# A new stored order of all five engines for a linear-attention and Fourier-mixing kernel

## The chip, the cores and the metric

The kernel runs on one core of a Trainium2 chip. Its metric is the time of one execution on the device in microseconds. The core has five engines that run on their own and meet through semaphores: TensorE (PE in the profile; its weight loads are PEld), VectorE (DVE), ScalarE (ACT), GpSimd (POOL) and SyncE (SP). SP issues nearly all transfers; POOL issues those of the two weight matrices.

## The reference, cut to what matters

```python
def _attn_ref(r, k, v, w, u):            # r, k, v, w: (4, 8, 768, 48); u: (8, 48)
    state = np.zeros((B, H, D, D))
    for t in range(S):
        cur = np.einsum('bhd,bhe->bhde', u[None] * kt, vt)
        y[:, :, t] = np.einsum('bhd,bhde->bhe', rt, state + cur)
        state = wt[:, :, :, None] * state + np.einsum('bhd,bhe->bhde', kt, vt)
    return y

def _moe_ref(x, w_ch1, w_ch2):           # x: (4, 768, 384), heads laid side by side
    X = np.fft.fft(np.fft.fft(x, axis=1), axis=2)
    u = x + np.real(X)
    un = (u - mean(u)) / np.sqrt(var(u) + 1e-06)      # over the last axis
    return u + np.maximum(un @ w_ch1, 0.0) @ w_ch2    # 384 -> 1536 -> 384
```

## The kernel before, in words

Four batches are worked one after another through the same stages, and the stages of neighbouring batches overlap.

*Attention.* The 768 steps of a batch are cut into six chunks of 128, one step per partition. For a chunk the decay w is turned into logarithms (ACT), summed over the steps by a matmul with a triangular matrix, and exponentiated (ACT). r and k are scaled by these (the tiles `rkh`, written by VectorE or POOL), transposed into `rkt` (by TensorE and an eviction, or by a transfer), and multiplied with each other (line 1120). A mask makes `ah` of the scores (line 1130, VectorE). The output of the chunk is `ah` times the values `vb` plus the transposed r times the state `st` (lines 1182 and 1185), plus the value times the scalar `dc`, the sum of r·k·u over a head: two products `rk` (VectorE or POOL), a reduction and a scaling `vtd`. The state goes from chunk to chunk (lines 1154, 1157, 1165).

Batch 0 is worked in pairs of chunks: its w, k and r come as three transfers of 384 KB for two chunks each (line 648); values, and all inputs of the other batches, come chunk by chunk in 192 KB (line 654). For each pair, `vec(2 * DM, tt(rk, rt, kt, ALU.mult), ...)` makes the product of r and k, in the profile `uf<-in_r,in_k` or `ht<-in_r,in_k` with 768 elements.

*Fourier mixing.* The outputs of chunks are folded with their mirror (tiles `sd` and `xf`, line 600 on VectorE or POOL), multiplied with tables of cosines and sines (lines 1261 to 1266), evicted to `hcs` with a mirrored copy `hcr`, and multiplied with tables of the second transform (line 1305, or 1314 in four parts). Input and result make `uf`; the normalized rows `un` are transposed to `unt`.

*The layer.* `unt` times W1 (line 1412, 288 matmuls) is evicted with a relu to `ht` (lines 1418 on VectorE and 1420 on ACT), and `ht` times W2 (line 1431) is evicted to `osb` and sent out. Half a batch is worked at a time.

*What sets the order.* The program first records every operation with a number, its reads and writes, the engines that may do it, and alternative forms of some steps (`choose`). A table of numbers, `ORDER`, then says for every engine which operations it does and in which order: `schedule` puts each operation on the engine in whose list its number stands, drops the forms that stand in no list, and gives PSUM banks; `emit` places the semaphore waits. Each engine works its list strictly from first to last. An operation of POOL also waits for the last VectorE instruction ahead of it in the plan that has two SBUF operands or could run in a faster mode.

At the very start TensorE has filler: sixteen matmuls on a tile of ones (line 1464) and `NW` more (line 1507). Ahead of the real work VectorE and ACT make masks and the tables of cosines and sines.

The names that matter below: line 600 is the helper for all elementwise operations on two tiles (`vec`), so VectorE's and POOL's shares of it are told apart by tile; line 639 is the load of u; line 402 and such are waits.

Of the kernel before, what the change touches and what calls it, by code (L numbers as in the profile page):

```python
# [31 lines left out]

W_AFTER = {"W1_0": (0, 4, "w")}

NW = 8

MEANS = (0,)


ORDER = {  # L40
# [26 lines left out]
    "act": (  # L67
# [15 lines left out]
    "dve": (  # L83
# [17 lines left out]
    "pool": (  # L101
# [13 lines left out]
}  # L115


# [335 lines left out]
def bass_rwkv6_finch__then__fnet_fourier_mix_kernel(  # L453
# [1048 lines left out]
    g.ctx = "warm"  # L1502
    for i in range(NW):
        t = g.tile("w")
# [36 lines left out]
```

## Time and profile before

| | |
|---|---|
| time, median of three runs | 179.47 us (179.09 to 179.93) |
| the profiled execution: time, span | 179.5 us, 177.3 us |
| PE busy | 171.9 us, 97% of the span |
| DVE busy | 157.8 us, 89% |
| ACT busy | 132.5 us, 75% |
| POOL busy | 98.4 us, 55% |
| PE clock granted | 1.000 |
| HBM read and written | 23.59 and 4.72 MB |

Times in the profile are microseconds from the start of the span. A busy engine is one that executes instructions; TensorE's matmuls overlap, so its busy time can hide gaps that are shorter than a matmul's way through the array. Idle time of an engine matters only where another engine waits for it.

### The profile page before, as it was taken

The numbers are of one execution on the slowest core, as the hardware profiler recorded it, in microseconds if no ns is written. First come the engines' busy times: TensorE is split into PE (matmuls) and PEld (weight loads), VectorE is DVE, ScalarE is ACT, GpSimd is POOL, SyncE is SP. The second block draws the span as 40 slices with busy tenths as digits, with TensorE's granted clock in tenths as the row PEclk, the third lists the DMA queues.
The fourth block names the chain that finished last, engine by engine and source line by source line (L and its number), as shares of the span: only waits on it lengthen the run. The fifth ranks groups of instructions, "written<-read, shape, count | busy, mean of one in ns | idle before, by whom it ended". The sixth has DMA issues, their size and how long they took to land.

```text
span 177.3 us, 4554 instructions
## 1 busy us (share of the span) xinstructions
PE 171.9 (97%) x1704; PEld 114.4 (65%) x1704; DVE 157.8 (89%) x379; ACT 132.5 (75%) x323; POOL 98.4 (55%) x127
## 2 busy tenths in 40 slices
PE   6998999999999999999999999999999999999994
PEld 3366667866766667776667667666666775665663
DVE  8979999999999999999999998999888999683443
ACT  2899999999999986999996988897924573602400
POOL 4024359759989557599589428899376124000000
DMA  5999999999999999997998969989983123240033
GB/s 131 296 276 246 211 202 190 184 177 215 188 186 163 161 186 217 211 208 151 205 191 168 239 134 207 171 150 243 210 174 102 50 89 67 46 154 4 0 133 133
DMA packets 109031, 29.55 MB, mean 167 GB/s; under 512 B 104273, under 2 KB 109010, under 8 KB 109010
## 3 DMA queue, kind: packets, MB, share of 16 engines
q1 hardware_dynamic: 107394, 26.91, 71.5%
q0 software_dynamic: 1616, 2.36, 8.5%
q8 instruction: 13, 0.21, 0.5%
q14 instruction: 8, 0.07, 0.1%
HBM read 23.59 MB, written 4.72 MB: 160 GB/s over the span
## 4 chain that ended last, share of the span: by engine, by line
PE 85%; DVE 6%; SPq 4%; DMA 3%; issue 1%; DVEq 0%
PE bank L1431 27%; PE bank L1412 27%; PE bank L1305 5%; PE bank L1261 3%; PE bank L1120 3%; DMA in_k<-in_k_dram 3%; SPq L648 3%; PE bank L1185 2%; PE bank L1182 2%; PE bank L992 2%; DVE rkh L600 2%; PE bank L1157 2%; PE bank L1109 2%; PE bank L1097 1%; DVE ah L1130 1%; PE bank L1015 1%
## 5 line engine op out<-in xcount | busy, mean ns | idle before, releaser
L1412 PE MATMUL bank<-unt,w 128*128 128x384 bf16 x288 | 53.5, 326 | 0.0
L1431 PE MATMUL bank<-w,ht 128*128 128x384 bf16 (+2 forms) x300 | 53.2, 320 | 0.0
L1420 ACT ACTIVATE ht<-bank 128x384 bf16<-128x384 f32 x75 | 35.2, 505 | 16.2 <-PE bank L1412 16.0
L1431 PEld LDWEIGHTS bank<-w,ht 128*128 128x128 bf16 x300 | 27.7, 98 | 15.7 <-issue 0.2
L1412 PEld LDWEIGHTS bank<-unt,w 128*128 128x128 bf16 x288 | 26.7, 98 | 15.7 <-DVE rkh L1046 0.2
L1130 DVE TENSOR_TENSOR ah<-bank,msk 128x512 bf16<-128x512 f32 x47 | 30.3, 678 | 1.6 <-PE bank L1120 1.3
L600 POOL TENSOR_TENSOR rk<-rk,ub 128x384 f32<-128x384 f32 x15 | 15.0, 1000 | 5.1 <-DVE rk L600 2.6
L1418 DVE TENSOR_SCALAR ht<-bank 128x384 bf16<-128x384 f32 x21 | 10.8, 548 | 7.0 <-PE bank L1412 7.0
L1440 DVE SCALAR_TENSOR_TENSOR osb<-bank,rstd,uf 128x384 f32<-128x384 f32 (+2 forms) x22 | 13.0, 591 | 4.0 <-DMA out_dram<-osb 2.4
L623 ACT ACTIVATE rkt<-bank 128x512 bf16<-128x512 bf16 (+1 forms) x22 | 15.5, 711 | 1.2 <-PE bank L1109 0.8
L614 ACT ACTIVATE un<-uf,agg 128x384 bf16<-128x384 f32 x22 | 12.8, 618 | 3.9 <-DVE agg L1364 3.9
L600 POOL TENSOR_TENSOR rkh<-in_k,e 128x384 bf16<-128x384 f32 x13 | 13.0, 1007 | 4.6 <-DVE xf L600 2.4
L600 POOL TENSOR_TENSOR vtd<-in_v,dc 128x384 f32<-128x384 f32 x17 | 14.0, 828 | 0.8 <-DVE dc L1064 0.7
L614 ACT ACTIVATE vb<-in_v 128x384 bf16<-128x384 f32 x23 | 12.3, 543 | 2.8 <-DMA in_v<-in_v_dram 2.8
L600 POOL TENSOR_TENSOR rk<-in_r,in_k 128x384 f32<-128x384 f32 x11 | 11.0, 1008 | 2.9 <-DVE xf L600 2.8
L1185 PE MATMUL bank<-vb,ah 128*128 128x48 bf16 x192 | 11.1, 183 | 0.0
L1185 PEld LDWEIGHTS bank<-vb,ah 128*128 128x128 bf16 x192 | 9.7, 96 | 1.6 <-issue 0.4
L600 POOL TENSOR_TENSOR sd<-x 128x385 f32<-128x385 f32 x8 | 8.0, 1008 | 4.6 <-DVE rkh L600 1.9
L1196 DVE TENSOR_TENSOR x<-bank,vtd 128x384 f32<-128x384 f32 x18 | 9.8, 547 | 0.8 <-PE bank L1185 0.5
L614 ACT ACTIVATE lb<-in_w 128x384 bf16<-128x384 f32 x18 | 9.8, 544 | 0.7 <-PE bank L992 0.4
L1362 DVE BATCH_NORM_STATS2 bst<-uf 128x6 f32<-128x384 f32 x18 | 9.6, 547 | 0.2 <-POOL uf L600 0.2
L1064 DVE TENSOR_REDUCE dc<-rk 128x8 f32<-128x384 f32 x18 | 9.7, 541 | 0.0
(208 smaller groups left out, 392.0 us busy)
## 6 DMA issues: line engine op xcount, KB each, us to landing
in_v<-in_v_dram SPq DMA_DIRECT2D x24, 192.0 KB, 4.4
out_dram<-osb SPq DMA_DIRECT2D x23, 192.0 KB, 2.6
in_w<-in_w_dram SPq DMA_DIRECT2D x18, 192.0 KB, 3.9
in_r<-in_r_dram SPq DMA_DIRECT2D x18, 192.0 KB, 3.8
in_k<-in_k_dram SPq DMA_DIRECT2D x18, 192.0 KB, 4.1
in_r<-in_r_dram SPq DMA_DIRECT2D x3, 384.0 KB, 4.4
in_k<-in_k_dram SPq DMA_DIRECT2D x3, 384.0 KB, 4.5
in_w<-in_w_dram SPq DMA_DIRECT2D x3, 384.0 KB, 5.4
```

The lines of the kernel that those rows point to most:

```text
L600: return lambda e: e.tensor_tensor(out=o, in0=a, in1=b, op=f)
L614: return lambda e: e.activation(o, a, f, **kw)
L623: {"act": lambda e: e.activation(o(), i(), ACTF.Copy), "dve": lambda e: e.tensor_copy(out=o(), in_=i())}, **kw)
L1064: op("dve", v_1(DM), lambda e: e.tensor_reduce(out=dc[:, :], in_=rku[:, :, :], axis=mybir.AxisListType.X, op=ALU.add), r=[("RK", i2)], w=[ ...
L1130: masked[n].append(op("dve", v_1(512), lambda e: e.tensor_tensor(out=ah[:, x:H:2, :], in0=ps(bk)[:, :].rearrange("p (h t) -> p h t", t=128 ...
L1185: ins = e.matmul(ps(ty)[:, D * h:D * h + D], ah[:, h, :], vb[:, h, :], start=first and not ype, stop=True, skip_group_check=True)
L1196: op("dve", v_1(DM), lambda e: e.tensor_tensor(out=xb[:, c, 0:DM], in0=ps(ty)[:, 0:DM], in1=vflat, op=ALU.add), r=[ty, ("VTD", n % 4)], w= ...
L1412: ins = e.matmul(ps(t)[:, 0:384], W1[:, m, 256 * (j // 2) + j % 2:256 * (j // 2) + 256:2], unt[:, :, m, :], start=(m == 0), stop=(m == NM ...
L1418: {"dve": lambda e, j=j, t=t, ht=ht: e.tensor_scalar(out=ht[:, j, :], in0=ps(t)[:, 0:384], scalar1=su, scalar2=0.0, op0=ALU.mult, op1=ALU. ...
L1420: "act": lambda e, j=j, t=t, ht=ht: e.activation(ht[:, j, :], ps(t)[:, 0:384], ACTF.Relu, scale=su)},
L1431: ins = e.matmul(ps(t)[:, 0:hi - lo], ht[:, j, 128 * x:128 * x + 128], W2[:, j, lo:hi], start=(j == 0), stop=(j == NJ - 1))
L1440: op("dve", v_1(hi - lo) + 64, lambda e: e.scalar_tensor_tensor(out=o[:, lo:hi], in0=ps(t)[:, 0:hi - lo], scalar=rstd[:, kb:kb + 1], in1=u ...
```

## The change

The table `ORDER` is replaced by another, and `NW` goes from 8 to 9. Everything else is the same text. The new table holds the lists of the five engines in another order, moves some operations to another engine, and picks another form for eight steps. It came from a search over the order, judged on mildly disturbed courses of the program's own plan.

```diff
-NW = 8
+NW = 9
 ORDER = {
     "pe": (
-        "8 84 2367 2368 2369 2370 2371 2372 2373 2374 105 108 101 208 211 204 102 77 138 157 151 152 155 147 "
...
+        "8 84 2367 2368 2369 2370 2371 2372 2373 2374 2375 108 105 101 211 208 204 102 77 155 138 157 151 152 "
...
     "sp": (
-        "87 83 86 82 90 88 92 91 95 89 97 93 96 636 638 687 98 94 789 99 738 689 637 639 845 688 690 790 739 "
...
+        "87 86 83 82 90 91 88 92 93 89 95 97 689 96 94 789 636 99 687 738 98 638 639 637 845 688 690 741 790 "
...
```

The steps with another form: the scaled k of chunks 2 and 3 (two operations of one chunk each become one of both), the sums of w for chunks 4 and 5 (one of the two running sums goes on in the bank of the first), the evictions of three transposes (two of 512 become one of 1024 for chunks 2 and 4 of batch 1, the reverse for chunk 1 of batch 2), the scaled r of chunk 5 of batch 3, the addition for chunk 1 of batch 3, and the output of the fourth block of batch 0.

The first place is the head of SP's queue. 128x8x96 is a transfer for two chunks of batch 0, 128x8x48 one for one chunk, 1x384 is u. Before:

```order
L648 DMA in_r<-in_r_dram 128x8x96
L639 DMA osb<-in_u_dram 1x384
L648 DMA in_k<-in_k_dram 128x8x96
L648 DMA in_w<-in_w_dram 128x8x96 x2
L654 DMA in_v<-in_v_dram 128x8x48
L648 DMA in_r<-in_r_dram 128x8x96
L648 DMA in_k<-in_k_dram 128x8x96
L648 DMA in_w<-in_w_dram 128x8x96
L654 DMA in_v<-in_v_dram 128x8x48
L648 DMA in_r<-in_r_dram 128x8x96
```

Now (the file is one line shorter, so lines count one less):

```order
L647 DMA in_r<-in_r_dram 128x8x96
L647 DMA in_k<-in_k_dram 128x8x96
L638 DMA osb<-in_u_dram 1x384
L647 DMA in_w<-in_w_dram 128x8x96 x2
L647 DMA in_k<-in_k_dram 128x8x96
L653 DMA in_v<-in_v_dram 128x8x48
L647 DMA in_r<-in_r_dram 128x8x96
L653 DMA in_v<-in_v_dram 128x8x48 x2
L647 DMA in_w<-in_w_dram 128x8x96
L647 DMA in_r<-in_r_dram 128x8x96
```

The k of chunks 0 and 1 now stands ahead of u, the k of chunks 2 and 3 ahead of the values of chunk 0 and of its own r, and the values of chunks 2 and 1 ahead of the w of chunks 4 and 5.

The second place is POOL's list in batch 3, around the scaled k of chunk 4 (`rkh<-in_k,e_1`). Before:

```order
L600 TENSOR_TENSOR rk<-in_r,in_k 128x384
L600 TENSOR_TENSOR rk<-rk,ub 128x384
L600 TENSOR_TENSOR uf<-uf,xf 128x191
L600 TENSOR_TENSOR rk<-rk,ub 128x384
L600 TENSOR_TENSOR uf<-uf,xf 128x191
L600 TENSOR_TENSOR rkh<-in_k,e_1 128x8x48
L600 TENSOR_TENSOR vtd<-in_v,dc 128x384 x2
L600 TENSOR_TENSOR x<-x,vtd 128x384
L600 TENSOR_TENSOR rk<-rk,ub 128x384
L600 TENSOR_TENSOR sd<-x 128x385
```

Now:

```order
L599 TENSOR_TENSOR uf<-uf,xf 128x191
L599 TENSOR_TENSOR vtd<-in_v,dc 128x384 x2
L599 TENSOR_TENSOR uf<-uf,xf 128x191
L599 TENSOR_TENSOR rk<-in_r,in_k 128x384
L599 TENSOR_TENSOR rk<-rk,ub 128x384
L599 TENSOR_TENSOR rk<-in_r,in_k 128x384
L599 TENSOR_TENSOR rkh<-in_k,e_1 128x8x48
L599 TENSOR_TENSOR x<-x,vtd 128x384
L599 TENSOR_TENSOR rk<-rk,ub 128x384
L599 TENSOR_TENSOR rk<-in_r,in_k 128x384
L599 TENSOR_TENSOR vtd<-in_v,dc 128x384
L599 TENSOR_TENSOR sd<-x 128x385
```

The products of r and k for chunks 4 and 5 of batch 3, which VectorE made before, now stand in POOL's list, one of them ahead of the scaled k of chunk 4, and two scalings `vtd` that stood behind it stand ahead of it.

133 rows, old and new, of the table ORDER are left out of this document.

## The prediction

> **What bounds the kernel now.** I read the head of the page first, then who TensorE waited for, then a table by stage, and last the chain of waits.
>
> ```profile
> span 177.3 us, 4554 instructions
> PE 171.9 (97%) x1704; PEld 114.4 (65%) x1704; DVE 157.8 (89%) x379; ACT 132.5 (75%) x323; POOL 98.4 (55%) x127
> ```
>
> TensorE is busy for 171.9 of 177.3 us. The profiled execution took 179.5 us, so 2.2 us lie around the span; the median of the runs is 179.47, which is the same. All sums below are made against 179.5. The view of waits lists everything for which TensorE's matmuls stood idle (who waited, for whom, us in total, times, longest):
>
> ```profile
> PE bank L1464 <- DVE w L611: 1.4, 1, 1.4
> PE bank L913 <- DVE sml L906: 0.3, 1, 0.3
> PE bank L1507 <- DVE msk L604: 0.3, 1, 0.3
> PE bank L942 <- DVE rkh L600: 0.3, 1, 0.3
> PE bank L1205 <- DVE vtd L600: 0.2, 1, 0.2
> PE bank L857 <- ACT uf L614: 0.2, 1, 0.2
> ```
>
> That is 2.7 us in all. The first 1.4 us stand ahead of the sixteen filler matmuls of line 1464, so no work of the kernel is late by them. The other lines all belong to batch 0 and the tables. The stages say the same (busy us of PE, weight loads, DVE, ACT, POOL in each stretch, then granted clock, DMA share and GB/s):
>
> ```profile
> 20.00:30.00 10.00, 9.86 (x141) 7.19 (x143) 10.00 (x19) 9.79 (x24) 6.68 (x13) 1.00 1.05 195
> 30.00:60.00 30.00, 29.99 (x360) 20.95 (x360) 29.37 (x74) 29.58 (x75) 25.52 (x31) 1.00 1.03 184
> 90.00:120.00 30.00, 30.00 (x341) 20.21 (x340) 28.82 (x63) 26.27 (x63) 22.46 (x25) 1.00 0.90 181
> 150.00:178.00 28.00, 24.80 (x165) 15.44 (x163) 14.10 (x31) 5.96 (x15) 0.59 (x1) 1.00 0.25 76
> ```
>
> From 30 us on TensorE has nothing left to win, and VectorE (DVE) runs within 0.63 us of full in 30 to 60 and within 1.18 us in 90 to 120. A new order of the same work can therefore gain almost only in the first 30 us, and can lose anywhere. The chain of waits tells what sets the opening (start, us, what), and how the end stands:
>
> ```profile
> 7.28 5.40 DMA in_k<-in_k_dram
> ...
> 13.64 1.02 DVE rkh L600 x2
> ...
> 24.24 0.48 DVE st L1165
> ...
> 146.17 5.20 PE bank L1431 x32
> ...
> 167.62 7.19 PE bank L1431 x56
> 174.91 0.35 DVE osb L1440
> ```
>
> The opening hangs on the eighth transfer of SP's queue, the keys of chunks 2 and 3. After it comes one unbroken string of VectorE instructions until 24.24. From there the chain is TensorE's, up to the last output.
>
> **The change part by part.** No computation goes. The count of TensorE's matmuls hardly moves: two fewer at line 857 and one more at line 863 for chunks 4 and 5, and one more filler at line 1507.
>
> *The opening transfers.* VectorE stands idle twice before 13 us, both times for keys:
>
> ```profile
> 6.16 0.96 DVE L600 TENSOR_TENSOR uf<-in_r,in_k 128x768 f32<-128x768 f32 x1 [0.32 <-DMA in_k<-in_k_dram]
> ...
> 10.85 0.96 DVE L600 TENSOR_TENSOR rkh<-in_k,uf 128x768 bf16<-128x768 f32 x1
> 12.77 0.96 DVE L600 TENSOR_TENSOR ht<-in_r,in_k 128x768 f32<-128x768 f32 x1 [0.96 <-DMA in_k<-in_k_dram]
> ```
>
> SP issues them like this:
>
> ```profile
> 1.25 0.47 SPq L639 DMA_DIRECT2D osb<-in_u_dram  x1
> 1.78 0.40 SPq L648 DMA_DIRECT2D in_k<-in_k_dram  x1
> ...
> 4.75 1.30 SPq L654 DMA_DIRECT2D in_v<-in_v_dram  x1
> 6.09 1.15 SPq L648 DMA_DIRECT2D in_r<-in_r_dram  x1
> 7.28 1.11 SPq L648 DMA_DIRECT2D in_k<-in_k_dram  x1
> ```
>
> The change issues the first keys ahead of the small load of u, at 1.25 instead of 1.78, 0.53 earlier. That can take away the first wait of 0.32, but alone it gives nothing: VectorE would then only stand longer at the second. For the second, the same eight transfers are ahead; the keys now go before the values and the receptances r of chunks 2 and 3, so r is the eighth. The lower bound of the gain is nothing, if the eighth lands at 12.68 (7.28 and 5.40) whatever it is. For the upper, the view of DMA issues has the median time from issue to landing in the first 16 us:
>
> ```profile
> in_r<-in_r_dram SPq DMA_DIRECT2D x3, 384.0 KB, 4.4
> in_w<-in_w_dram SPq DMA_DIRECT2D x3, 384.0 KB, 5.4
> in_v<-in_v_dram SPq DMA_DIRECT2D x3, 192.0 KB, 4.5
> ```
>
> An r issued at 7.28 with 4.4 lands at 11.68, before VectorE is free (10.85 and 0.96 is 11.81). Then both waits go: 0.32 and 0.96 are 1.28. Between 0 and 1.28 I take 0.6, about the middle, since the bytes ahead are the same, and the 5.40 of this transfer against the usual 4.4 shows that it was late for a reason I can't see. The string of VectorE behind it holds the same work: up to the product of chunk 5 with its mask, at 31 us, VectorE's instructions differ by one tiny scaling taken from ACT and a few fills. So the gain goes on to TensorE.
>
> *What the transfers push back.* The first values, now seventh, are issued about where r stood, at 6.09, and land with 4.5 at 10.6. The decay w of chunks 4 and 5 goes from ninth to eleventh place behind two more small loads; issued two places later, where the trace issues at 10.51, it lands with 5.4 at 15.9. ACT uses them here:
>
> ```profile
> 10.44 0.53 ACT L614 ACTIVATE vb<-in_v 128x384 bf16<-128x384 f32 x1
> ...
> 10.51 2.17 SPq L648 DMA_DIRECT2D in_r<-in_r_dram  x1
> ...
> 15.65 0.83 ACT L614 ACTIVATE uf<-in_w 128x768 bf16<-128x768 f32 x1
> ```
>
> So ACT may wait 0.16 and 0.25, and behind the first wait stand the exponentials that the products of chunks 0 and 1 need. I count 0.1 on the path; bounds are 0 (the products wait for r anyway) and 0.4.
>
> *Forms and fillers.* A matmul of 384 columns leaves every 0.163 us (32 in 5.20). One fewer of them at lines 857 and 863 and one more filler at 1507 cancel. The filler stands where TensorE waits for line 857 anyway; with that cover gone it would cost its 0.163. Sum 0.
>
> *Work moved from VectorE to POOL.* Counted over both programs, the products r times k go from 7 on VectorE and 11 on POOL to 3 and 15, one sum of two chunks and one addition of 191 columns move too.
>
> ```profile
> L600 POOL TENSOR_TENSOR rk<-in_r,in_k 128x384 f32<-128x384 f32 x11 | 11.0, 1008 | 2.9 <-DVE xf L600 2.8
> ...
> L600 DVE TENSOR_TENSOR rk<-in_r,in_k 128x384 f32<-128x384 f32 x7 | 3.8, 548 | 0.0
> ...
> L600 POOL TENSOR_TENSOR uf<-uf,xf 128x191 f32<-128x191 f32 x8 | 4.7, 590 | 5.6 <-DVE uf L1353 2.9 <-DVE uf L600 2.6
> ```
>
> POOL gets about 5 times 1.0 and 0.6, which is 5.6 us; VectorE loses 4 times 0.548, about 0.55 for the sum and 0.36 for the addition, 3.1 us. Nearly all of it lies after 70 us, where TensorE never waits, so the gain there is close to 0. POOL is 55% busy; in 90 to 120 it has 7.5 us free. What hides the longer POOL instructions is that the products are wanted only by the reduction to dc and the scaled values, which the output of a chunk needs last. I take 0, with a gain of 1.5 (half of the relief, if VectorE is the hidden bound) and a loss of 1.5 (below) as bounds.
>
> What POOL can cost is seen where its instruction meets one of VectorE that also reads two tiles of SBUF:
>
> ```profile
> 147.60 0.36 DVE L600 TENSOR_TENSOR uf<-uf,xf 128x191 f32<-128x191 f32 x1
> ...
> 148.83 1.14 POOL L600 TENSOR_TENSOR uf<-uf,xf 128x191 f32<-128x191 f32 x2 [0.20 <-DVE uf L1353]
> ...
> 149.46 0.72 DVE L600 TENSOR_TENSOR uf<-uf,xf 128x191 f32<-128x191 f32 x1
> ```
>
> The same addition took 0.36 alone and 0.72 while POOL was busy until 149.97: VectorE was held. The Trainium skill, page "SBUF — State Buffer", section "Who interferes with whom", has the rule: a VectorE instruction with two SBUF inputs and a GpSimd instruction that reads SBUF exclude each other for the whole instruction, and whoever comes first goes first. This row agrees with it. By that rule each moved product is a stretch of 1.0 in which such VectorE work stands still, which speaks against the change; it is the first rival.
>
> *The turn to batch 3 and the end.* The 32 matmuls from 146.17 bridge the time in which batch 3 is normalized and transposed. In the new order the same nine groups of four output matmuls (32 in that row and four just before it) bridge it again. The last 7.19 us of TensorE are one run of output matmuls before and after. I count 0 for both.
>
> **Sum.** 179.5 minus 0.6 plus 0.1 is 179.0 us.
>
> **The rivals.** *POOL holds VectorE.* About six more POOL instructions stand where VectorE is nearly full. Each that meets a two-input instruction costs 0.36 (the row) to 1.0. Four meetings at 0.36 are about 1.5, past the 0.6 gained, and TensorE waits for masks and sums. Time: 179.0 and 1.5, 180.5. For it: no slack on VectorE between 30 and 120. Against: the relief of 3.1 us, and POOL's idle times before its products show that the order already keeps the two apart. It decides from two meetings on the path.
>
> *Both keys' waits go.* r lands after 4.4 and ACT's loads come in time: 179.5 minus 1.28 is 178.2. For it: 4.4 is the median. Against: the engines of the DMA are full.
>
> *VectorE was the bound of the middle.* Then half of the 3.1 us, 1.5, comes off beside the 0.6 and the 0.1: 177.5. For it: 29.37 of 30. Against: no wait of TensorE there.
>
> *The new order does nothing for the time.* The eighth transfer lands as before and the rest cancels: 179.5.
>
> **How the numbers follow.** What a measurement can tell from no change is about 0.5%, 0.9 us. Forecast 179.0, own range 178.5 to 179.5: 0.37. POOL holds VectorE, 180.5: 0.21. Both waits go, 178.2: 0.20. VectorE's bound, 177.5: 0.10. Nothing, 179.5: 0.12. Faster by over 0.9 us are the third (most of it) and the fourth, and a little of the first: 0.33. Slower are most of the second and a tail of the last: 0.22. The rest, 0.45, is the same. The range from 177.6 to 180.8 reaches into the two outer cases.
>
> **What would show it.** The product r times k of chunks 2 and 3 (VectorE, 12.77 now) starts at 11.5 to 12.5, and the string behind it is as long as now; if it starts at 12.7 the first term is wrong. ACT's first conversion of v starts no later than 10.8. TensorE's waits after 30 us stay under 0.3; VectorE's additions and products that read two tiles stay at 0.55, and longer ones mean the first rival. The wait before batch 3's first matmul of line 1412, at 151, stays away. A new wait of TensorE between 30 and 150 of more than half a microsecond would make the prediction wrong.

## The result and the profile after

| | before | after |
|---|---|---|
| time, median of six runs | 179.32 us (178.88 to 179.93) | 178.13 us (177.88 to 178.17) |
| after over before, 95% interval | | 0.9932 (0.9914 to 0.9949) |
| the profiled execution: time, span | 179.5, 177.32 us | 178.16, 176.35 us |
| what lies around the span | 2.2 us | 1.8 us |

The change is faster by 1.2 us, 0.7%. The forecast was 179.0 with a range from 177.6 to 180.8, and 178.1 lies inside it. It lies outside the 178.5 to 179.5 that the prediction gave to its own course of things, and beside the rival at 178.2. The head of the page of the changed kernel, and all of its waits of TensorE's matmuls:

```profile
span 176.3 us, 4538 instructions
PE 171.6 (97%) x1704; PEld 114.4 (65%) x1704; DVE 155.7 (88%) x372; ACT 133.0 (75%) x324; POOL 103.7 (59%) x131
```

```profile
PE bank L1463 <- DVE w L610: 1.3, 1, 1.3
PE bank L856 <- ACT uf L613: 0.6, 1, 0.6
```

The first wait is the one ahead of the fillers. The second is new in its size, but stands ahead of line 856 with fillers on its other side; the logarithms that it waits for come at the same time as before, so nothing is late by it. After 30 us no wait is left, as before. Now VectorE's start of the program (start, us, the instruction; what ended a wait would stand in brackets):

```profile
5.55 0.19 DVE L603 TENSOR_SCALAR msk<-osb 128x128 bf16<-128x128 f32 x1
...
5.87 0.93 DVE L599 TENSOR_TENSOR uf<-in_r,in_k 128x768 f32<-128x768 f32 x1
...
10.82 0.94 DVE L599 TENSOR_TENSOR rkh<-in_k,uf 128x768 bf16<-128x768 f32 x1
...
11.69 0.95 DVE L599 TENSOR_TENSOR ht<-in_r,in_k 128x768 f32<-128x768 f32 x1
...
30.82 0.54 DVE L1164 TENSOR_TENSOR st<-bank,sml 128x384 bf16<-128x384 f32 x1
```

Both waits for keys are gone. The product of r and k of chunks 2 and 3 (`ht<-in_r,in_k`, called the product below) starts at 11.69 instead of 12.77, directly behind the instruction before it. The string behind it holds: the last update of batch 0's state starts at 30.82, and stood at 31.80 before:

```profile
31.80 0.54 DVE L1165 TENSOR_TENSOR st<-bank,sml 128x384 bf16<-128x384 f32 x1
```

The chain of waits of the changed kernel shows that TensorE carries this to the end. Its first row here ends with the landing of r at 11.18, 0.5 us before the product that reads it, so no engine stood for it:

```profile
6.57 4.61 DMA in_r<-in_r_dram
...
145.20 5.20 PE bank L1430 x32
...
166.44 7.41 PE bank L1430 x56
```

The 32 output matmuls that bridge the turn to batch 3 start at 145.20 instead of 146.17, and the last run of TensorE ends at 173.85 instead of 174.81: 0.96 earlier, the whole of the 1.0 us that the span lost. Three of the stages shown in the prediction say that the middle is as full as it was:

```profile
20.00:30.00 10.00, 9.99 (x141) 6.84 (x140) 10.00 (x21) 10.00 (x26) 6.78 (x11) 1.00 1.05 188
30.00:60.00 30.00, 29.95 (x356) 21.33 (x355) 29.49 (x70) 29.85 (x79) 25.60 (x32) 1.00 1.06 191
90.00:120.00 30.00, 30.00 (x351) 20.35 (x350) 28.98 (x62) 25.86 (x64) 22.75 (x26) 1.00 1.06 180
```

In the profiled executions, then, 1.0 us of the gain lies in the opening, and 0.4 us lies around the span (0.3 us by the medians below).

### The profile page after: what moved, and what is told of

The parts are those of the page before. It is cut to its first block, busy times and chain, and to the rows that moved or that the text cites. A ratio compares the mean times of both kernels' runs of the same rounds, so it can differ in the third digit from the quotient of the medians.

```text
span 176.3 us, 4538 instructions
## 1 busy us (share of the span) xinstructions
PE 171.6 (97%) x1704; PEld 114.4 (65%) x1704; DVE 155.7 (88%) x372; ACT 133.0 (75%) x324; POOL 103.7 (59%) x131
## 4 chain that ended last, share of the span: by engine, by line
PE 87%; DVE 4%; SPq 3%; DMA 3%; issue 1%; DVEq 0%
PE bank L1430 27%; PE bank L1411 27%; PE bank L1304 5%; PE bank L1119 4%; PE bank L1260 4%; DMA in_r<-in_r_dram 3%; PE bank L1184 3%; SPq L647 2%; PE bank L1181 2%; PE bank L1204 2%; PE bank L1156 2%; PE bank L991 2%; PE bank L1108 2%; PE bank L1265 1%; PE bank L1014 1%; DVE ah L1129 1%
## 5 line engine op out<-in xcount | busy, mean ns | idle before, releaser
L1419 ACT ACTIVATE ht<-bank 128x384 bf16<-128x384 f32 x74 | 33.8, 494 | 10.8 <-PE bank L1411 10.5
L1439 DVE SCALAR_TENSOR_TENSOR osb<-bank,rstd,uf 128x384 f32<-128x384 f32 (+2 forms) x23 | 13.5, 593 | 7.7 <-PE bank L1430 7.4
L599 POOL TENSOR_TENSOR rk<-in_r,in_k 128x384 f32<-128x384 f32 x15 | 15.0, 1002 | 4.7 <-DVE rk L599 2.4
L1417 DVE TENSOR_SCALAR ht<-bank 128x384 bf16<-128x384 f32 x22 | 11.6, 547 | 6.3 <-PE bank L1411 5.9
L622 ACT ACTIVATE rkt<-bank 128x512 bf16<-128x512 bf16 (+1 forms) x21 | 14.8, 740 | 2.5 <-PE bank L1108 2.5
L599 POOL TENSOR_TENSOR sd<-x 128x385 f32<-128x385 f32 x9 | 8.9, 1009 | 1.7 <-DVE x L1195 1.1
L1181 PE MATMUL bank<-st,rkt 128*128 128x96 bf16 x80 | 9.7, 204 | 0.0
L1195 DVE TENSOR_TENSOR x<-bank,vtd 128x384 f32<-128x384 f32 x17 | 9.2, 548 | 0.4 <-PE bank L1184 0.3
```

Source lines behind the costliest of these rows:

```text
L599: return lambda e: e.tensor_tensor(out=o, in0=a, in1=b, op=f)
L622: {"act": lambda e: e.activation(o(), i(), ACTF.Copy), "dve": lambda e: e.tensor_copy(out=o(), in_=i())}, **kw)
L1181: e.matmul(ps(ty)[:, 96 * q:96 * q + 96], rT[:, q, :], s_in[:, q, :], start=not ype, stop=False, skip_group_check=True)
L1417: {"dve": lambda e, j=j, t=t, ht=ht: e.tensor_scalar(out=ht[:, j, :], in0=ps(t)[:, 0:384], scalar1=su, scalar2=0.0, op0=ALU.mult, op1=ALU. ...
L1419: "act": lambda e, j=j, t=t, ht=ht: e.activation(ht[:, j, :], ps(t)[:, 0:384], ACTF.Relu, scale=su)},
L1439: op("dve", v_1(hi - lo) + 64, lambda e: e.scalar_tensor_tensor(out=o[:, lo:hi], in0=ps(t)[:, 0:hi - lo], scalar=rstd[:, kb:kb + 1], in1=u ...
```

## The experiments

Line numbers in the experiments' profiles are 12 above those of before (14 in the two with fills of an unused tile; the changed kernel run again has its own). Besides its median, each kernel is told by the median span of its executions and by what the device time has beyond the span, since the two move apart. Times of before in the three sets were 179.39, 179.41 and 179.46 us. Four single executions are left out: one of 608 us in the second run with both keys early, one of 183.9 us in the run with the second keys and the mask, and two of before in the first set, 181.2 and 183.1 us (the 179.39 still counts these two).

### Which transfer gives the gain

In SP's list, 87 and 86 are r and k of chunks 0 and 1, 83 is u, 82 and 90 are the w, 88 the first values, 92 and 91 r and k of chunks 2 and 3. Both keys early, in the order of before:

```diff
-        "87 83 86 82 90 88 92 91 95 89 ...
+        "87 86 83 82 90 91 88 92 95 89 ...
```

> The order of before, with only the head of SP's queue taken from the change: both keys early. Theory A (the head of SP's queue is the whole gain): VectorE has 0.32 + 0.96 us of waits to lose, and no other one appears, so the product of r and k of chunks 2 and 3 starts at 11.7 to 11.9 instead of 12.77 and the time falls by 0.9 to 1.1 us. Theory B (the gain needs the new lists of the other engines too: VectorE's lists of the first 12 us were written for the old landings): the product may start as early, but the time falls by less than 0.5 us, because other waits open between 12 and 30 us.

Measured: 178.53 us, ratio 0.9954 (0.9938 to 0.9969), median span 176.4 against 177.2. VectorE has no wait left ahead of the product:

```profile
11.53 0.95 DVE L612 TENSOR_TENSOR ht<-in_r,in_k 128x768 f32<-128x768 f32 x1
```

Only the first keys:

```diff
-        "87 83 86 82 90 88 92 91 95 89 ...
+        "87 86 83 82 90 88 92 91 95 89 ...
```

> The order of before, with only the first keys put ahead of the small load of u. Theory A1 (the small load in second place holds the whole stream of transfers back: the first keys landed at 6.07 in the profile of before and at 5.35 in that of after, 0.72 earlier): everything behind lands 0.5 to 0.7 us earlier, the second keys at 12.0 to 12.2, and the time falls by 0.5 to 0.7 us. Theory A2 (of the prediction: alone it gives nothing, VectorE only stands longer at the second keys): second keys at 12.6 to 12.7, time as before within 0.2 us.

Measured: 178.84 us, ratio 0.9973 (0.9952 to 0.9993), median span 176.7.

Only the second keys:

```diff
-        "87 83 86 82 90 88 92 91 95 89 ...
+        "87 83 86 82 90 91 88 92 95 89 ...
```

> The order of before, with only the second keys moved ahead of the values and the r of chunks 2 and 3, so that r is the eighth transfer. If the eighth transfer lands when it lands, whatever it is: r at 12.7, product at 12.8, time as before within 0.2 us. If the eighth was late for a reason of its own (5.40 us against 4.4 for r), r lands at about 11.7 to 12.0 and the time falls by 0.6 to 0.9 us; the wait of 0.32 for the first keys stays in both cases.

Measured: 179.37 us, ratio 1.0001 (0.9974 to 1.0029). The twelve executions spread from 178.44 to 180.34: five lie from 178.4 to 178.9, where both keys early lie, and six from 179.5 to 180.3.

And the other way, the changed kernel with the old head of the list:

```diff
-        "87 86 83 82 90 91 88 92 93 89 ...
+        "87 83 86 82 90 88 92 91 93 89 ...
```

> The changed kernel, with only the first eight transfers of SP in the old order. Theory A (the head is the whole gain): both waits of VectorE come back, the product starts at 12.6 to 12.8, and the time is 0.9 to 1.2 us above the changed kernel, level with before. Theory C (the other lists gain by themselves, by half of the work taken from VectorE): the time stays 0.3 us or more below before.

Measured: 178.87 us, ratio 0.9974 (0.9949 to 0.9999), median span 177.05. Its profile is of the longest of the twelve executions (179.27). Both waits are back in it:

```profile
6.52 0.96 DVE L612 TENSOR_TENSOR uf<-in_r,in_k 128x768 f32<-128x768 f32 x1 [0.57 <-DMA in_k<-in_k_dram]
...
12.91 0.96 DVE L612 TENSOR_TENSOR ht<-in_r,in_k 128x768 f32<-128x768 f32 x1 [0.61 <-DMA in_k<-in_k_dram]
```

By the spans, the head of the list is worth about 0.8 us alone (177.2 to 176.4), and 0.7 us when it is taken out of the change (from 176.3 and 176.4 in the two runs of the changed kernel, on other chips, to 177.05). So it is nearly all that the span gained. The profiles say the same more closely. In eleven of the thirteen profiled executions (without the one of 608 us) the span is 164.5 to 164.9 us longer than the start of the product, whether that stands at 11.5 or at 12.9. The two others are the run with products taken back to VectorE (165.5) and the one with fills on POOL (165.2), both described below. The changed kernel with the old head is still 0.5 us below before, but 0.3 of this lies around the span; the fourth part takes that up.

The first keys alone bring 0.5 us. The prediction had said that they bring nothing, because VectorE would only stand longer at the second keys. Its two rows in that run show why not:

```profile
10.64 0.96 DVE L612 TENSOR_TENSOR rkh<-in_k,uf 128x768 bf16<-128x768 f32 x1
11.80 0.96 DVE L612 TENSOR_TENSOR ht<-in_r,in_k 128x768 f32<-128x768 f32 x1 [0.20 <-DMA in_k<-in_k_dram]
```

The second keys are the eighth transfer here too, and were issued at 6.53 instead of 7.28, but they are waited for only until 11.80. So the eighth transfer is not late by its place alone; u in second place has a part in it: with u ahead of the first keys SP issues the eighth transfer at 7.23 to 7.65 (five profiles), with u behind them at 6.44 to 6.65 (eight profiles). The trace also has a landing for each of the sixteen parts into which a transfer is split, and the engine waits for the last of them:

```
                          first   last    spread (us)
before, first keys        5.02    6.07    1.05
before, first w           6.23    7.27    1.04
before, second keys      11.12   12.68    1.56   (14 of the 16 by 11.78, two at 12.59 and 12.68)
after, first keys         4.92    5.35    0.43
after, first w            6.14    6.55    0.41
after, r of chunks 2, 3  10.76   11.17    0.41
only the first keys early:
  first keys              4.80    5.35    0.55
  second keys            10.52   11.70    1.18   (15 of the 16 by 11.22)
```

The first parts land at nearly the same time in both kernels. With the load of u (1.5 KB) between r and the keys, the last part of the first keys lands 0.72 later, and the spread stays near 1 us in the next three transfers. The other profiles agree: the spread of the first keys is 1.05 to 1.45 in the five with u ahead of them and 0.41 to 0.67 in the eight with u behind. That the small load delays only some of the parts is seen; what it does in the queues, and why SP then issues the eighth transfer later, is not.

At the eighth transfer, r landed at 11.66 and 11.90 with u ahead of the keys (the third run here, and one below), at 10.99 and 11.17 with u behind them (the first run, and the changed kernel): 0.5 to 0.9. The keys as the eighth landed at 12.68, 12.82 and 12.00 with u ahead (before, the fourth run, one below), at 11.70 with it behind. The keys thus come somewhat later than r in the same place. Counted from the issue, r took 4.37 to 4.67 in this place, in nine profiles, with u ahead or behind; the keys took 4.77 to 5.40 in four, one of them with u behind (5.17). So moving u brings the issue forward, and putting r last shortens the way from issue to landing. Why the keys take longer in this place stays open; in before two of their sixteen parts are 0.8 behind the other fourteen.

### Why the second keys alone gave nothing in the median

The profile of that run is of one of the six longer executions (179.72). VectorE's product there stood behind an instruction that waited for ACT, not for a transfer, and ACT waited for TensorE:

```profile
11.87 0.96 DVE L612 TENSOR_TENSOR rkh<-in_k,uf 128x768 bf16<-128x768 f32 x1 [0.95 <-ACT uf L898]
12.74 0.95 DVE L612 TENSOR_TENSOR ht<-in_r,in_k 128x768 f32<-128x768 f32 x1
```

TensorE's rows of the same execution, and the stretches with the granted clock (third figure from the right):

```profile
1.43 4.07 PE L1476 MATMUL bank<-w 128*128 128x384 bf16 x16 [1.43 <-DVE w L623]
...
5.43 0.91 PE L719 MATMUL bank<-osb,vtd 1*128 1x384 f32 x2
7.53 2.74 PE L1519 MATMUL bank<-idw,msk 128*128 128x384 bf16 x8 [1.19 <-DVE msk L616]
```

```profile
6.00:7.00 1.00, 0.34 (x2) 0.00 (x0) 0.83 (x1) 0.98 (x2) 0.00 (x0) 1.00 1.17 324
7.00:8.00 1.00, 0.47 (x2) 0.28 (x3) 1.00 (x8) 0.91 (x2) 0.00 (x0) 0.76 1.11 306
8.00:9.00 1.00, 1.00 (x5) 0.45 (x3) 1.00 (x5) 1.00 (x3) 0.00 (x0) 0.50 1.16 303
9.00:10.00 1.00, 1.00 (x4) 0.45 (x3) 1.00 (x4) 0.75 (x2) 0.41 (x1) 0.50 1.20 274
10.00:11.00 1.00, 1.00 (x5) 0.47 (x4) 0.92 (x6) 0.06 (x1) 0.81 (x3) 0.53 1.08 291
```

The same rows of before:

```profile
1.43 4.96 PE L1464 MATMUL bank<-w 128*128 128x384 bf16 x16 [1.43 <-DVE w L611]
...
7.52 1.48 PE L1507 MATMUL bank<-idw,msk 128*128 128x384 bf16 x8 [0.29 <-DVE msk L604]
```

The sixteen fillers ended at 5.50 here, and at 6.39 in the profile of before. So TensorE stood idle for 1.19 us until the mask that the next fillers read, and VectorE made that mask only behind its wait for the first keys. At the end of the idle time the granted clock fell to 0.50, and the eight fillers took 2.74 us; in before they took 1.48. The trace's record of the clock has full speed from 4.11 to 7.52 and half speed from 7.52 to 10.93, 3.41 us each. The matmuls of the sums came 0.9 late (10.06 instead of 9.16). The Trainium skill, page "TensorE: Matmul & The Clock Gate", section "What's actually happening", puts the half clock behind at least one idle window of about 3.4 us. The stretches here have that length, but the one ahead of the fall was not idle: it held 1.39 us of the first fillers and 0.91 us of two matmuls on one row, beside the 1.19 us of idling. A stretch with less idling passed: in the run with fills on POOL below, the first fillers ended at 5.68, TensorE stood idle for 0.59 us behind the same two matmuls, and the clock stayed at full.

In the changed kernel this mask is made at 5.55, ahead of the first keys (its row is shown above). In before it stood behind them:

```profile
7.24 0.22 DVE L604 TENSOR_SCALAR msk<-osb 128x128 bf16<-128x128 f32 x1
```

To tell the mask from the transfer, it was moved alone and with the second keys (28 is the mask, 135 the first product):

```diff
-        "... 135 43 28 29 36 ...
+        "... 28 135 43 29 36 ...
```

> Before with only the second keys early, and the mask that TensorE's fillers wait for made ahead of VectorE's first wait for keys instead of behind it. Theory G (without the mask the second keys gave nothing because TensorE stood idle for 1.2 us, ran the next matmuls at half speed and was 0.9 us late): the wait of line 1507 and the slow matmuls go, no execution lies above 179.3, and the median is 178.5 to 178.8, 0.6 to 0.9 us below before. Theory T (the transfers gave nothing): the median stays at 179.2 to 179.4.

Measured: 178.67 us, ratio 0.9957 (0.9935 to 0.9980), executions from 178.39 to 179.27, median span 176.5. The product starts at 11.99, behind r:

```profile
11.99 0.96 DVE L612 TENSOR_TENSOR ht<-in_r,in_k 128x768 f32<-128x768 f32 x1 [0.31 <-DMA in_r<-in_r_dram]
```

> Before with only that mask made ahead of VectorE's first wait. Theory G: VectorE's second wait for keys (0.96 us) stays and sets the time, so the median falls by 0.3 us at most, but the executions of before above 179.7 us (granted clock 0.99 in most of them on one chip) go away. Rival: the median falls by 0.5 us or more, and then the gain of the change is the mask's, not the keys'.

Measured: 179.51 us, ratio 1.0008 (0.9984 to 1.0032), executions from 178.89 to 180.77.

So the second keys are worth 0.8 us as soon as the mask is out of the way, and the mask by itself moves the median not at all. The expectation on the tail was half right: none of these twelve executions has a granted clock under 0.995, where 6 of the 32 of before beside them have, but five of the twelve are still above 179.7. One stretch of 3.41 us at half speed makes a mean of 0.99 over a span of 177 us. Over all the runs such a mean stands in 13 of 94 executions with u ahead of the keys and the mask behind them (10 of before, 3 with the second keys alone), and in 1 of 111 of the other kernels, of which 36 have u ahead and the mask early; the one is the execution of 183.9 us that is left out above, with the mask early. Chips differ: of before's 35 executions in the first set none has it. The clock is thus one cause of longer executions, and another stays open. In the run with the second keys alone, three of the six executions above 179.5 have a granted clock of 0.99, and the other three are not explained. One thing that varies is the landing of the eighth transfer: with the same list of SP the keys landed at 12.00 in the profile with the mask early, of the shortest of its executions, and at 12.68 in that of before.

The gains of the two keys don't add up: the first 0.5, the second (with the mask) 0.8, both 0.8 to 0.9. With both early VectorE has no gap left ahead of the product; with the first alone a wait of 0.20 is left in the profile, and with the second keys and the mask waits of 0.19 and 0.31.

### What the moved products are worth

The changed kernel with five products of r and k put back on VectorE, and the order of before with both keys early and the same five put on POOL; both original kernels ran beside them.

```diff
 the changed kernel
-    "pool": ( ... 1320 ... 1427 ... 1482 ... 2003 ... 2058 ...
+    "dve": ( ... 1320 1256 ... 1427 1308 ... 1482 1402 ... 2003 1721 ... 2058 2021 ...
 the order of before with both keys early
-    "dve": ( ... 1320 ... 1427 ... 1482 ... 2003 ... 2058 ...
+    "pool": ( ... 1320 1269 ... 1427 1444 ... 1482 1494 ... 2003 2058 1838 ...
```

> The order of before with both keys early once more, to stand beside the changed kernel on the same chip: 0.8 to 0.9 us below before.

Measured: ratio 0.9947 (0.9926 to 0.9968), five executions from 178.54 to 178.83, median span 176.6. The profile of this run fell on the execution that is left out, so none is shown.

> The changed kernel with five products of r and k (chunks 2, 4 and 5 of batch 2, chunks 4 and 5 of batch 3) taken back from POOL to VectorE, which gets 5 times 0.55 = 2.7 us more work. If the move was worth nothing (the prediction's 0): level with the changed kernel within 0.3 us. If VectorE is a hidden bound of the middle: slower than the changed kernel by 0.4 to 1.4 us. If POOL's products held VectorE: faster than the changed kernel by 0.3 us or more.

Measured: 178.95 us, ratio 0.9968 (0.9952 to 0.9985), median span 177.1.

> The order of before with both keys early, and the same five products moved from VectorE to POOL; everything else stays. If the move is worth nothing: level with the kernel with both keys early within 0.3 us. If VectorE is a hidden bound: faster than it by 0.4 us or more (half of the 2.7 us, 1.4, at most). If POOL holds VectorE: slower by 0.4 to 1.5 us, and VectorE's two-operand instructions in 70 to 135 us become longer than 0.55.

Measured: 178.05 us, ratio 0.9921 (0.9899 to 0.9944), median span 176.2.

> The changed kernel once more beside the others. If the head of SP's queue is the whole gain, it is level with the kernel of before with both keys early within 0.2 us; if the other lists bring the rest of the measured 1.2 us, it is 0.3 to 0.5 us below it.

Measured: 178.19 us, ratio 0.9918 (0.9899 to 0.9937), median span 176.4.

In the old order, the five products on POOL leave the span where it was in the profiled executions, both among the shortest of their runs. The chain of waits of the first run (both keys early, products on VectorE) has these rows, and that of the run with the products on POOL has the very same:

```profile
145.09 5.20 PE bank L1443 x32
...
166.54 7.19 PE bank L1443 x56
```

TensorE is at the same place to a hundredth; compared one by one, none of its 1704 matmuls stands more than 0.2 us off, and that only among the fillers. Over all executions the median spans are 176.4 with the products on VectorE (27 executions, with the fills below counted in) and 176.3 with them on POOL (13). So the move is worth nothing there that can be told from the spread. The exclusion that the first rival feared was there: two of VectorE's instructions on two tiles of SBUF took 1.30 and 1.13 instead of 0.55 while POOL worked. First VectorE's rows, then POOL's:

```profile
124.65 1.30 DVE L612 TENSOR_TENSOR rkh<-in_k,e 128x384 bf16<-128x384 f32 x1 [0.18 <-DMA in_k<-in_k_dram]
...
127.27 1.13 DVE L612 TENSOR_TENSOR rk<-rk,ub 128x384 f32<-128x384 f32 x1
128.32 0.55 DVE L612 TENSOR_TENSOR sd<-x 128x385 f32<-128x385 f32 x1
```

```profile
124.54 0.99 POOL L612 TENSOR_TENSOR rk<-in_r,in_k 128x384 f32<-128x384 f32 x1 [0.90 <-DVE rkh L612]
...
126.99 1.00 POOL L612 TENSOR_TENSOR x<-x,vtd 128x384 f32<-128x384 f32 x1
```

In the whole of this profile VectorE's instructions of this kind are stretched at four places by 2.1 us, in that of both keys early at three by 0.6. So of the 2.7 us taken from VectorE its busy time shows only 0.7 (158.0 to 157.3): the stretching takes most of the relief back, and TensorE feels neither.

In the new order, taking the products back costs 0.7 us of span (176.4 to 177.1). Against the profile of the second run of the changed kernel, TensorE is 0.2 us late by 78 us, 0.4 by 100, 1.1 by 135, and 0.9 at the end. Most of it comes between 131 and 135 us:

```profile
134.27 0.25 PE L1273 MATMUL bank<-ss,xf 128*128 128x193 bf16 x1
134.83 0.22 PE L1194 MATMUL bank<-st,rkt 128*128 128x96 bf16 x1 [0.31 <-DVE ah L1142]
```

The wait in the row is 0.31 of it; 0.22 more stands inside the sixteen score matmuls before, which took 0.84 instead of 0.62 (in their middle the weight loads wait for a state of VectorE). The masked blocks of the row are VectorE's, with no idle time ahead of them in this run:

```profile
132.44 0.53 DVE L1076 TENSOR_REDUCE dc<-rk 128x8 f32<-128x384 f32 x1
132.90 2.47 DVE L1142 TENSOR_TENSOR ah<-bank,msk 128x512 bf16<-128x512 f32 x4
```

In the changed kernel (its second run) VectorE was there early enough to wait for the scores:

```profile
130.75 0.54 DVE L1063 TENSOR_REDUCE dc<-rk 128x8 f32<-128x384 f32 x1
131.74 2.48 DVE L1129 TENSOR_TENSOR ah<-bank,msk 128x512 bf16<-128x512 f32 x4 [0.44 <-PE bank L1119]
```

So the new order uses the room that the move made: the same five products are worth nothing that can be told from the spread in one order, and 0.7 in the other, where taking them back gives VectorE 2.1 us more busy time (155.8 to 157.9).

### The 0.3 us around the span

In these runs and the earlier ones the time beyond the span falls in two groups, whatever the span is: 2.13 to 2.17 us with before, with the keys early in any way, and 1.81 to 1.84 with the changed kernel, with the old head in it, with its products back on VectorE, and with the products on POOL in the old order. The end is alike in all: the last transfer lands 0.5 us before the span ends. To see whether the length of a program makes it, eight tiny fills of an unused tile were added to POOL, and to VectorE:

```diff
+    PAD = sb("pad", [NPAD, 3], FP32)
+    for i in range(NPAD):
+        op("pool", 60, fill(PAD[:, i, :], 0.0), w=[("PAD", i)])
```

> The order of before with both keys early, and eight tiny fills of an unused tile at the end of POOL's list, where POOL is idle. The time beside the span was 2.13 to 2.16 us in every kernel with the old lists of VectorE and POOL and 1.81 to 1.84 in every kernel with five products moved or with the new lists. If POOL's longer program makes that 0.3 us: 1.8 here, and a time 0.3 us below the kernel without the fills (178.2). If VectorE's shorter program makes it, or something else: still 2.15, time 178.5 to 178.8.

Measured: 178.74 us, 2.17 us around the span; ratio 0.9960 (0.9943 to 0.9978).

> The order of before with both keys early and the five products on POOL, and eight tiny fills of an unused tile between VectorE's evictions after 157 us, where VectorE is idle half of the time. If VectorE's shorter program made the time beside the span fall from 2.15 to 1.84: back at 2.15, time 178.3 to 178.4. If POOL's longer program made it, or something else: still 1.84, time 178.0 to 178.1.

Measured: 178.11 us, 1.81 us around the span; ratio 0.9940 (0.9918 to 0.9962).

Neither moves it. In the first, POOL has as many instructions in the trace as in the changed kernel (168); in the second, VectorE has as many as in before (441, where before has 439). What goes with the two groups by count is TensorE's program: beside its matmuls it has 1778 instructions in the profiles of all seven kernels of the first group, and 1774 to 1777 in those of the five of the other. That was not tried, and it can be chance; the cause stays open.

## Why the prediction was right, and which terms were off

**The bound.** Right. The gain in the span is in the first 30 us, TensorE carries it unchanged to the last output, and no wait of TensorE came up after 30 us.

**The opening transfers, 0.6 of 1.28.** The main mechanism was right: product at 11.69 within 11.5 to 12.5, string as long as it was. The size was too small. By the spans the head is worth 0.7 to 0.8, and against the profiled execution of before 1.08 in VectorE's start. The step that failed is "alone it gives nothing" for the first keys, with the eighth transfer taken as issued at 7.28 in the new order too. Alone the first keys gave 0.5. Putting u behind them brought the issue of the eighth forward, to 6.53 with the first keys alone and 6.57 in the changed kernel, and narrowed the spread of the first keys' landings, from 1.05 to 0.55 and 0.43 us. The eighth landed at 11.70 with the first keys alone, against 12.68 in before and 12.00 in another execution with before's list of SP. The other step, 4.4 from issue to landing for an r in eighth place, was nearly right: it took 4.60. The reason for 5.40 against 4.4, which the prediction could not see, goes with the keys in that place and stays open.

The rival with both waits gone, 178.2, describes the profile of the changed kernel: r landed at 11.17, before VectorE was free.

**What the transfers push back, 0.1.** Nothing. The first values landed at 9.92, and w of chunks 4 and 5 at 14.61, both before ACT came to them:

```profile
10.41 0.53 ACT L613 ACTIVATE vb<-in_v 128x384 bf16<-128x384 f32 x1
...
15.55 0.88 ACT L613 ACTIVATE uf<-in_w 128x768 bf16<-128x768 f32 x1
```

They stood at 10.44 and 15.65. The error was of the same kind: issue and landing were carried over from the old stream, and the new one ran ahead of it (the w was issued at 9.68, where the prediction took 10.51).

**Forms and fillers, 0.** Not measured alone; TensorE's 1704 matmuls stayed. What the prediction did not see is that the mask ahead of the fillers was moved before the first keys, where, by the counts above, it seems to keep the stretch at half clock away (13 of 94 executions against 1 of 111). In the old order it moves no median by itself.

**Work from VectorE to POOL, 0.** Right in the old order, where the span did not move clear of its spread, and so both rivals built on it fall there: POOL holds VectorE for 2.1 us in all, and TensorE does not wait for it; what is left of VectorE's relief is worth nothing. In the changed kernel the sign that the prediction named for the first rival did appear, two of VectorE's instructions longer than 0.55 while POOL worked:

```profile
101.22 0.73 DVE L599 TENSOR_TENSOR xf<-sd 128x384 bf16<-128x384 f32 x1
...
103.46 1.02 DVE L599 TENSOR_TENSOR rkh<-in_k,e 128x384 bf16<-128x384 f32 x1
```

No wait of TensorE followed, so it is the price of that rival that was wrong, not its mechanism. VectorE's busy time fell by 2.1 us, where the prediction counted 3.1. But the term stands in the new order, and there the move is needed: undone, it costs 0.7. To cost a moved operation in the old order's slack is not the same as in the order it comes with.

**The turn and the end, 0.** Right: 32 output matmuls at 145.20, the first matmuls of batch 3 follow them without a wait, 0.97 before their old time.

**The sum.** 0.75 for the head and 0.1 to 0.2 for the rest of the new order in the span, and 0.33 around it, make the 1.2. The prediction had 0.5, and had taken what lies around the span as fixed at 2.2; that part of the miss is the 0.33 and has no shown cause. Part of the agreement with the rival at 178.2 is therefore luck: the span alone would have given 178.5, the edge of the prediction's own range.

No kernel here clearly beats the change. The old order with both keys early and five products on POOL, 178.05, is level with it, 178.19: two keys brought forward and five products moved in the old table reach what the whole new table does, and 0.3 us of that is the part around the span.

## What to carry to other kernels

When an engine waits for the last of a row of transfers, look at the parts of the earlier ones: in this kernel a small load between large ones spread them and held the later ones back. Try the small load in a later place, and try the two halves of such a change apart, since the gain of one can be hidden by a wait elsewhere (here a mask that stood behind the very wait). What work taken from a nearly full engine is worth depends on the order around it, so test it in the order in which it will stand.

## What the runs showed of the hardware that was not expected

- A transfer of 1.5 KB between two of 384 KB spread the sixteen landings of the next one over 1.05 to 1.45 us in five profiles, against 0.41 to 0.67 in eight with it one place later; in before the spread stayed near 1 us for three more transfers.
- TensorE's granted clock fell to 0.50 behind a stretch of 3.41 us with 1.19 us of idling in it, and stayed there for 3.41 us: eight matmuls took 2.74 instead of 1.48 us.
- The sixteen fillers from 1.43 ended at 5.50 in one execution, at 6.39 in another of nearly the same order. Both start a filler every 0.32 us at first and every 0.16 later; the turn came at 4.1 in the one, where the record of the clock begins to show full speed, and at about 5.9 in the other.
- The device time beyond the span was 2.15 or 1.82 us by program, in the same way on three chips.
